# More of the first MoE's opening piece inside the attention's instruction list, with the list and the piece groups rearranged

## The chip, the cores and the metric

The program runs on one core of one Trainium2 chip. The metric is device time in microseconds, the median of the runs of one program; lower is better. Before the change three runs gave 1019.2 to 1020.21 us with a median of 1019.82 us.

## What is computed

The inputs are double precision. An attention over 4 batches, 8 heads, 576 positions and head size 64 comes first, then two feed-forward layers over the 2304 tokens:

```python
bias = -(cum[:, :, :, None] - cum[:, :, None, :])
scores = np.where(causal, -1e9, scores + np.minimum(bias, 0.0))
attn = softmax(scores); x = attn @ v            # 2304 tokens x 512
x = (sigmoid(x @ w_gate) * (x @ w_val)) @ w_out   # MoE 1: 512 -> 1536 -> 512
h = x @ w_in; out = (h * np.cos(h)) @ w2_out      # MoE 2: 512 -> 2048 -> 512
```

## The kernel before, in words

Every product of the two MoE layers is made of three float32r matmuls (`mm3`, lines 390 to 393): high half by high half, high by low, low by high. So each activation and each weight is kept as a high and a low tile. The weights come as doubles; a piece of 128 columns (or rows) is fetched (L302) and decoded by `piece_ops`: VectorE takes out the exponent (L306) and the mantissa (L314, L318), adds the sign (L322) and makes the high half (L332), ScalarE shifts the exponent (L310), GpSimd joins them (L326) and makes the low half (L336).

**Attention.** The 32 heads are worked as 16 pairs p = 0 to 15, four pairs to a batch. The steps of a pair are scores (A), mask (Z, ZA, ZM, on GpSimd mostly), row minimum (X, VectorE, L694), exponential (E, ScalarE, L698), transposes (T, TensorE, L481), copies of them (C, ScalarE or VectorE), the product with v (V, TensorE, L768 and L770), its copy out (U), the reciprocal of the row sums through DRAM (RA, RC, RT, RR, RD, RB), the division (M) and the split into `XH` (XH) and `XL` (XL). All of it, with the decoding of the first three weight pieces (w0, w1, w2), stands in one hand-ordered list, the string `SEQ`: each word is a step, a letter behind the colon the engine that takes it (a: ScalarE, d: VectorE, p: GpSimd). Each engine runs its steps in the order of the list. `Plan.run` (L200 on) gives the PSUM banks while it goes through the list; PSUM has eight banks, and nearly all steps of the attention take two neighbouring ones.

**MoE 1.** Tokens are cut into six blocks of 384. The 12 pieces of 128 hidden columns go in groups (`GROUPS1`, L372); a group runs over all six blocks, and within a block over its pieces. An item (block, piece) has 12 matmuls for the gate, 12 for the value and 12 for the four downs (36 in all). After the last piece of a group each of the four down banks is taken out (`evac1`): in the first group copied to `acc` by ScalarE (L937), in later ones added to it by VectorE (L939). While a group runs, `background` decodes the weight pieces of the next one, a few steps per item. TensorE's order in an item i is: gate and value of i, then the downs of i-1. VectorE's is: multiply value and gate of i (L909), additions of the first two down banks, low half (L917), additions of the other two, decoding.

At the end of the list stand the first parts of MoE 1: gate and value of the first two items (I0 to I15, each three matmuls), the sigmoid chain of the first (Gs, Gm, Gh, Gl) and its four downs (D0 to D3). They sit on fixed banks, all of them among the last steps of pairs 14 and 15. `moe()` goes on with item 2.

Of the kernel before, what the change touches and what calls it, by code (L numbers as in the profile page):

```python
# [10 lines left out]
F32 = mybir.dt.float32  # L11
# [166 lines left out]
WARM = 11  # L178
W0AT = 2
# [18 lines left out]
C0.2.3:d ZA0.5 A3.5 E0.4.4 ZT1.5 HQ6:d ZM0.3.5 C1.2.3:a M1:p E1.2.4 T0.3.4 RT3 GV3 X0.3.5 XH1:p T1.3.4 RR3:a DB6 X1.3.5 GK7 C0.3.4:a ZA1.5 XL1:d A4.5 A0.5 T0.4.4 C1.3.4:a
X1.0.5 X0.0.5 E0.3.5 ZM1.2.5 X1.1.5 RB2 C0.4.4:d V0.3 V1.3 E1.3.5 ZT0.6 X0.1.5 Z1.6:p A2.5 E0.2.4 E1.1.5 ZT1.6 E0.0.5 E0.1.5 T0.2.4 ZM0.2.5 T1.2.4 RA4 Z0.6:p E1.0.5 U3:d
RD3 T0.1.5 ZM0.3.6 ZA1.6 C0.2.4:a ZM1.3.6 X0.2.5 X1.2.5 T0.0.5 A5.5 ZA0.6 RC4 GQ7 PK7 X0.4.5 M2:p C1.2.4:a C0.1.5:a A3.6 RT4 C0.0.5:a T0.3.5 HK7:d DB7 E0.4.5 RR4:d X1.3.6  # L200
T1.3.5 X0.3.6 E0.2.5 A4.6 C0.3.5:a A0.6 X0.1.6 C1.3.5:a T0.4.5 GV5 E1.2.5 A2.6 XH2:p X1.0.6 X1.1.6 ZM1.2.6 ZM0.2.6 RB3 GKT8 RA5 C0.4.5:a X0.0.6 RC5 RD4 T0.2.5 T1.2.5
E1.1.6 XL2:d V0.4 GK8 E0.0.6 Z0.7:p E1.3.6 Z1.7:p E0.1.6 ZT0.7 C0.2.5:d E1.0.6 X1.2.6 X0.2.6 E0.3.6 C1.2.5:d V1.4 U4:a PQ7 T0.0.6 DB8 ZM0.3.7 T0.1.6 C0.1.6:a GQT8 ZA0.7
A5.6 RT5 HQ7:d T0.3.6 T1.3.6 X0.4.6 C0.0.6:a ZT1.7 RR5:d PK8 E0.4.6 A3.7 T0.4.6 HK8:d X0.3.7 M3:p ZA1.7 ZM1.3.7 X1.3.7 w0fetch RB4 C0.3.6:a C1.3.6:a ZM1.2.7 C0.4.6:a A4.7
RD5 E0.2.6 E1.2.6 A0.7 E1.3.7 X0.1.7 PQ8 XL0:p Z1.8:p GQ9 X1.0.7 GVT8 V0.5 HQ8:d X1.1.7 X0.0.7 E0.1.7 w0exponent V1.5 GV6 XH3:d U5:d E0.3.7 A2.7 E1.1.7 ZM0.2.7 E1.0.7 RA6
Z0.8:p ZM0.3.8 X0.2.7 E0.0.7 T0.2.6 T1.2.6 GQ11 T0.1.7 T0.0.7 ZM1.3.8 X1.2.7 C1.2.6:a C0.2.6:a ZT0.8 A5.7 C0.1.7:a w0mant_hi X0.4.7 ZT1.8 PK9 RC6 HK9:a C0.0.7:d A3.8
X0.3.8 RT6 T0.3.7 M4:p E0.4.7 T1.3.7 DB9 GV7 PQ9 X1.3.8 RR6:a C0.3.7:a ZA1.8 ZA0.8 A4.8 E0.3.8 A0.8 C1.3.7:d w0mant_lo E0.2.7 X1.0.8 X1.1.8 ZM1.2.8 X0.0.8 X0.1.8 V0.6
T0.4.7 E1.2.7 HQ9:a XL3:p GK11 E1.1.8 E0.0.8 w0rebias GQ10 Z0.9:p E0.1.8 T0.2.7 w0sign Z1.9:p C0.4.7:d ZM0.2.8 T1.2.7 RA7 C0.2.7:d V1.6 C1.2.7:d ZT0.9 E1.0.8 A2.8 ZT1.9
E1.3.8 X0.2.8 RB5 U6:a T0.1.8 ZM0.3.9 T0.0.8 E0.2.8 A5.8 A3.9 X1.2.8 PQ10 X0.4.8 ZA1.9 C0.1.8:a RD6 X0.3.9 ZM1.3.9 C0.0.8:a T0.3.8 ZA0.9 X1.3.9 M5:p T1.3.8 HQ10:a w1fetch
GK10 XH5:p A4.9 DB10 C1.3.8:d w0add_exp A0.9 E0.3.9 V0.7 E1.3.9 X0.1.9 X0.0.9 X1.1.9 XL5:p X1.0.9 RB6 RC7 XH4:p C0.3.8:d E1.2.8 w0split_hi E0.4.8 E0.1.9 PK10 E1.1.9
# [12 lines left out]
E1.2.12 T0.2.12 XL9:d w1split_hi E0.3.13 ZM0.2.13 E0.0.13 V0.11 E1.0.13 w2fetch X1.2.13 X0.2.13 C0.2.12:d RA12 XH8:d V1.11 w1split_lo M10:p E1.1.13 U11:d T1.2.12 E0.1.13
T0.0.13 C1.2.12:d T0.1.13 A5.13 ZA1.14 X0.4.13 Z1.14:a E0.2.13 E0.4.13 GK15 PQ15 C0.1.13:d DB15 V0.12 w2exponent E1.3.13 HQ15:d RC12 C0.0.13:a E1.2.13 V1.12 XL8:p RT12
T0.4.13 T0.2.13 T1.2.13 w2mant_hi RA13 RR12:d U12:a T0.3.13 RB11 C0.4.13:d ZA0.14 A4.14 Z0.14:p C0.2.13:a A0.14 C0.3.13:a ZT0.15 C1.2.13:d T1.3.13 GV13 ZA0.15 XH10:a RD12
RC13 ZM0.3.14 A3.14 ZT1.15 X0.0.14 X1.1.14 X1.0.14 C1.3.13:a ZM1.3.14 X0.1.14 X1.3.14 X0.3.14 PK15 w2rebias E0.0.14 XL10:p GV14 ZM1.2.14 ZM0.2.14 E1.3.14 V0.13 E0.1.14
HK15:d E1.0.14 w2mant_lo E1.1.14 RT13 A2.14 Z0.15:p V1.13 X1.2.14 E0.3.14 Z1.15:p RR13:a T0.0.14 T0.1.14 X0.2.14 U13:a A4.15 ZA1.15 A0.15 M11:p C0.1.14:a X0.1.15 X1.0.15
# [9 lines left out]
def kernel(  # L236
# [188 lines left out]
    def attention():  # L425
        with ExitStack() as c2:
# [401 lines left out]
            for i, it in enumerate(items1[0:2]):  # L828
# [8 lines left out]
                if i:  # L837
                    continue
# [312 lines left out]
```

## Time and profile before

| what | value |
|---|---|
| median of three runs | 1019.82 us |
| the profiled execution, its own time | 1018.92 us |
| its span (first to last instruction) | 1017.1 us |
| TensorE busy | 1005.4 us, 99% |
| weight loads busy | 913.3 us, 90% |
| VectorE, ScalarE, GpSimd busy | 713.8, 476.2, 408.7 us |
| granted TensorE clock | 0.999 |
| end of the last product with v | 169.75 us into the span |

The program has two stages: the list (the attention), to about 172 us, and the two MoE layers behind it. In the profile a matmul's end is modelled, and one that follows closely overlaps the next; so the distance from one start to the next tells what a matmul costs, not the busy time alone.

### The profile page before, as it was taken

Reading aid. Unit: us, or ns where it says so; the run is one execution under the profiler, and the core shown is the slowest. Engines: PE = TensorE matmul, PEld = TensorE weight load, DVE = VectorE, ACT = ScalarE, POOL = GpSimd, SP = SyncE. Lnnn points to the kernel's source line nnn. Section 1 sums busy time; section 2 is a strip of 40 time slices with the busy share of each in tenths; the row PEclk is TensorE's granted clock in tenths of the full one; section 3 lists DMA queues with packets and bytes.
Section 4 is the critical chain, followed back from the end, with each engine's and each line's share of the span. In section 5 each row is a group of like instructions: output and inputs, shape, how many; then the busy total and the mean of one; then the engine's idle time right before and its main releaser. Section 6 shows DMA issues by size and latency. Waiting matters only on the chain.

```text
span 1017.1 us, 17408 instructions
## 1 busy us (share of the span) xinstructions
PE 1005.4 (99%) x6553; PEld 913.3 (90%) x6553; DVE 713.8 (70%) x1369; ACT 476.2 (47%) x1079; POOL 408.7 (40%) x484
## 2 busy tenths in 40 slices
PE   8999999999999999999999999999999999999998
PEld 5666668999999999999999999899999999999997
DVE  7789885956556577633435878987688888876665
ACT  6998986522122122222112345665555455454453
POOL 5477875532212223311111225555255536552222
PEclk9999999999999999999999999999999999999999
DMA  8988762311111112201001121111012101100011
GB/s 185 201 200 208 189 157 78 103 56 48 44 42 42 42 60 65 64 21 39 24 21 42 42 63 53 52 63 42 22 42 63 42 21 53 52 1 32 32 63 62
DMA packets 91509, 69.43 MB, mean 68 GB/s; under 512 B 58849, under 2 KB 79713, under 8 KB 91425
## 3 DMA queue, kind: packets, MB, share of 16 engines
q1 hardware_dynamic: 89792, 67.86, 24.1%
q8 instruction: 51, 0.84, 0.3%
q10 hardware_dynamic: 1632, 0.47, 0.2%
q14 instruction: 34, 0.27, 0.1%
HBM read 63.45 MB, written 4.87 MB: 67 GB/s over the span
## 4 chain that ended last, share of the span: by engine, by line
PE 85%; DVE 2%; ACT 1%; issue 1%; DMA 0%; POOL 0%; DVEq 0%; POOLq 0%; ACTq 0%
PE pw L391 21%; PE pw L392 21%; PE pw L393 21%; PE pw L992 6%; PE pw L991 6%; PE pw L993 6%; PE pw L770 1%; PE pw L481 1%; PE pw L658 1%; PE pw L663 1%; DMA raw<-in_moe_w_gate_dram 0%; DVE pu L694 0%; DVE wm L314 0%; ACT pu L698 0%; DVE wx L306 0%
## 5 line engine op out<-in xcount | busy, mean ns | idle before, releaser
L391 PE MATMUL pw<-XH,wp 128*128 128x384 f32 x960 | 322.9, 336 | 0.0
L392 PE MATMUL pw<-XL,wp 128*128 128x384 f32 x960 | 322.7, 336 | 0.0
L393 PE MATMUL pw<-XH,wp 128*128 128x384 f32 x960 | 322.6, 336 | 0.0
L336 POOL TENSOR_TENSOR wp<-wm,wp 128x512 fp32r<-128x512 f32 x68 | 100.9, 1483 | 222.1 <-DVE wp L332 218.5
L391 PEld LDWEIGHTS pw<-XH,wp 128*128 128x128 f32 x960 | 180.1, 188 | 4.0
L392 PEld LDWEIGHTS pw<-XL,wp 128*128 128x128 f32 x960 | 180.0, 188 | 3.6
L393 PEld LDWEIGHTS pw<-XH,wp 128*128 128x128 f32 x960 | 180.1, 188 | 0.0
L326 POOL TENSOR_TENSOR wm<-wm,wx 128x512 int32<-128x512 int32 x68 | 90.5, 1331 | 176.3 <-DVE wm L322 175.5
L981 POOL TENSOR_TENSOR gpb<-tmb,gpb 128x384 fp32r<-128x384 f32 x72 | 82.8, 1150 | 110.4 <-ACT gpb L980 110.4
L909 DVE TENSOR_TENSOR tmb<-pw,tmb 128x384 f32<-128x384 f32 x57 | 31.7, 556 | 114.0 <-PE pw L393 111.6
L310 ACT ACTIVATE wx<-wx,ebias 128x512 int32<-128x512 int32 x68 | 49.3, 725 | 92.6 <-DVE wx L306 91.5
L698 ACT ACTIVATE pu<-pu,nm 128x256 f32<-128x256 f32 (+4 forms) x144 | 83.2, 582 | 5.9 <-DVE nm L694 5.7
L992 PE MATMUL pw<-wp,gpb 128*128 128x512 f32 x216 | 84.1, 389 | 0.0
L991 PE MATMUL pw<-wp,gpb 128*128 128x512 f32 x216 | 84.1, 389 | 0.0
L993 PE MATMUL pw<-wp,gpb 128*128 128x512 f32 x216 | 84.0, 389 | 0.0
L391 PE MATMUL pw<-gpb,wp 128*128 128x384 f32 x216 | 72.6, 336 | 1.0 <-ACT acc L937 1.0
L392 PE MATMUL pw<-gpb,wp 128*128 128x384 f32 x216 | 72.9, 337 | 0.0
L393 PE MATMUL pw<-gpb,wp 128*128 128x384 f32 x216 | 72.2, 334 | 0.0
L322 DVE SCALAR_TENSOR_TENSOR wm<-raw,wm 128x512 int32<-128x512 int32 x68 | 69.1, 1017 | 1.5
L960 ACT ACTIVATE tmb<-pw 128x384 int32<-128x384 f32 x96 | 46.6, 485 | 37.6 <-PE pw L393 37.4
L911 ACT CAST gpb<-tmb 128x384 fp32r<-128x384 f32 x43 | 22.1, 514 | 88.7 <-DVE tmb L909 88.7
L908 ACT ACTIVATE tmb<-pw 128x384 f32<-128x384 f32 x57 | 27.8, 488 | 72.4 <-PE pw L393 72.3
(134 smaller groups left out, 1889.9 us busy)
## 6 DMA issues: line engine op xcount, KB each, us to landing
raw<-in_moe_w_out_dram SPq DMA_DIRECT2D x28, 512.0 KB, 3.5
CB<-cum_d SPq DMA_DIRECT2D x15, 576.0 KB, 4.5
raw<-in_moe_w_in_dram SPq DMA_DIRECT2D x16, 512.0 KB, 3.7
raw<-in_moe_w_gate_dram SPq DMA_DIRECT2D x12, 512.0 KB, 3.4
raw<-in_moe_w_val_dram SPq DMA_DIRECT2D x12, 512.0 KB, 3.4
rb<-rec_d SPq DMA_DIRECT2D x32, 144.0 KB, 3.3
out_dram<-acc SPq DMA_DIRECT2D x17, 256.0 KB, 2.1
Kn<-in_k_dram SPq DMA_DIRECT2D x16, 256.0 KB, 5.8
```

What stands on the lines that cost most here:

```text
L310: act.activation(x, x, AF.Relu, bias=ebias[e], scale=8.0)
L322: dve.scalar_tensor_tensor(m, st["raw"][:, :, 1], -2**31, m, ALU.bitwise_and, ALU.bitwise_or)
L326: pool.tensor_tensor(m, m, st["x"], ALU.add)
L336: pool.tensor_tensor(w[:, 1], st["m"].bitcast(F32), f(w[:, 0]), ALU.subtract)
L391: pe.matmul(ps, wh, xh, start=first, stop=False)
L392: pe.matmul(ps, wh, xl, start=False, stop=False)
L393: pe.matmul(ps, wl, xh, start=False, stop=last)
L698: act.activation(o, o, AF.Exp, bias=NMT[nm.slot][:, col:col + 1], scale=-1.0, accum_out=SUMS[sums.slot][:, col:col + 1])
L981: pool.tensor_tensor(gl, g, f(gh), ALU.subtract)
L991: pe.matmul(ps, gh[:, ts], w[:, 0], start=it["first"], stop=False)
L992: pe.matmul(ps, gh[:, ts], w[:, 1], start=False, stop=False)
L993: pe.matmul(ps, gl[:, ts], w[:, 0], start=False, stop=it["last"])
```

## The change

Gate and value of the first four items instead of two, and the downs of the first two instead of one, now stand in the list, scattered from pair 12 on. They take single free PSUM banks that the plan gives out, not fixed ones. The list is ordered anew as a whole. The gate of these four items is made with `Exp`, an addition and a reciprocal on VectorE, not with `Sigmoid`. The tiles for the high and low halves (`GH`, `GL`) lie where the attention's q and k were, and are made once the last of these has been transposed. The last pair takes its reciprocals in a tile of `pt` and not in `rb`; the tail of v has one tile, not two. `GROUPS1` has seven groups: the second one has a single piece. In `moe()` items 2 and 3 start with their splits and downs, on the banks that the list's downs leave, and item 4 makes gate and value of chunks 0 to 2 first and of chunk 3 last. `acc`, `tma`, `tmb`, `gpa` and `gpb` become tiles of their own per block or slot.

```diff
+NI = 4
-    GROUPS1 = [[0], [1, 2], [3, 4], [5, 6], [7, 8, 9], [10, 11]]
+    GROUPS1 = [[0], [1], [2, 3], [4, 5], [6, 7], [8, 9], [10, 11]]
...
-            for i, it in enumerate(items1[0:2]):
-                i_ps = Buf(pl["pw"], 2, 2 * i)
+            for i, it in enumerate(items1[0:NI]):
+                ig, iv = Buf(pl["pw"], 1), Buf(pl["pw"], 1)
...
-                    act.activation(g, it["ps"][0], AF.Sigmoid)
+                    act.activation(g, PW[:, ig.slot, 0:it["n"]], AF.Exp, scale=-1.0)
+                def glu_m(u, it=it, g=TM[i], iv=iv):
+                    dve.tensor_scalar(g, g, 1.0, None, ALU.add)
+                    dve.reciprocal(g, g)
+                    dve.tensor_tensor(g, PW[:, iv.slot, 0:it["n"]], g, ALU.mult)
...
+                if i == NI:
+                    for ks in (range(NDC - 1), [NDC - 1]):
+                        for ps, z in ((pg, "g"), (pv, "v")):
+                            xmm(ps, W[z, it["f"]], it["o"], it["n"], ks)
...
                 if i == 0:
                     ahead()
+                    for k, x in enumerate(items1[2:NI]):
+                        glu(x)
+                        glu_lo(x)
+                        for z, (y, c, _) in enumerate(downs[4 * k:4 * k + 4]):
+                            evac1(items1[y], c, z % 2)
+                    for k, x in enumerate(items1[2:NI]):
+                        for c in range(NDC):
+                            down1(x, c)
+                        for c in range(NDC):
+                            evac1(x, c, c % 2)
+                        if k == 0:
+                            background(5)
```

TensorE at pair 12, before: the transpose of the reciprocals of pair 10 (`rc`), then scores (`K`, `Q`), transposes (`pu`) and the product with v (`pt`, `VN`).

```order
L481 MATMUL pw<-ident,rc 9x64 x2
L658 MATMUL pw<-K_83,Q_81 128x512 x2
L481 MATMUL pw<-ident,pu_104 128x64 x10
L663 MATMUL pw<-K_83,Q_81 128x288 x2
L658 MATMUL pw<-K_83,Q_81 128x128 x2
L658 MATMUL pw<-K_83,Q_81 128x256 x2
L768 MATMUL pw<-pt_105,VN_108 64x64 x2
```

The same place in the change (`wp` is a weight tile; L393 to L395 are the three matmuls of a part of MoE 1).

```order
L395 MATMUL pw<-XH,wp 128x384
L488 MATMUL pw<-ident,rc 9x64 x2
L488 MATMUL pw<-ident,pu_109 128x64 x10
L669 MATMUL pw<-K_89,Q_87 128x288 x2
L664 MATMUL pw<-K_89,Q_87 128x128 x2
L664 MATMUL pw<-K_89,Q_87 128x256 x2
L590 MATMUL pw<-ident,Kn_94 128x64 x8
L590 MATMUL pw<-ident,Kt 128x64 x2
L393 MATMUL pw<-XH,wp 128x384
```

Parts of MoE 1 now stand between the steps of pair 12; before, the first of them stood among the last steps of pairs 14 and 15. Over the whole list they came in five runs on TensorE (4, 5, 2, 5 parts and the 4 downs) and come in nine now (3, 5, 4, 1, 3, 13, 3 parts, 1 down, 7 downs).

TensorE at the end of the list, before: the products with v of the last two pairs (`pt_105`, `pt_106`), then the downs (`gpa`).

```order
L770 MATMUL pw<-pt_106,VN_108 64x448 x2
L770 MATMUL pw<-pt_105,VN_107 64x320 x2
L770 MATMUL pw<-pt_105,VN_107 64x192 x2
L770 MATMUL pw<-pt_105,vt_110 64x64 x2
L770 MATMUL pw<-pt_106,VN_108 64x320 x2
L770 MATMUL pw<-pt_106,VN_108 64x192 x2
L770 MATMUL pw<-pt_106,vt_110 64x64 x2
L391 MATMUL pw<-gpa,wp 128x384
```

And in the change:

```order
L488 MATMUL pw<-ident,rc 9x64 x2
L393 MATMUL pw<-gh_2651,wp 128x384
L394 MATMUL pw<-gl_2655,wp 128x384
L395 MATMUL pw<-gh_2651,wp 128x384
L774 MATMUL pw<-pt_111,VN_113 64x64 x2
L776 MATMUL pw<-pt_111,VN_113 64x512 x2
L776 MATMUL pw<-pt_111,VN_113 64x448 x2
L776 MATMUL pw<-pt_111,VN_113 64x320 x2
L776 MATMUL pw<-pt_111,VN_113 64x192 x2
L776 MATMUL pw<-pt_111,vt 64x64 x2
L393 MATMUL pw<-gh_2651,wp 128x384
```

One down stands before the last product with v and seven behind it; the product of pair 14 has moved up. Ahead of the last product with v stood 48 matmuls of MoE 1; now 99 stand there (96 and 3).

VectorE in the second group of MoE 1, before (`tmb<-pw` is the multiplication, `acc` the additions, `wx`, `wm` and `wp` are decoding):

```order
L909 TENSOR_TENSOR tmb<-pw,tmb 128x384
L939 TENSOR_TENSOR acc<-pw,acc 128x384 x2
L917 TENSOR_TENSOR gpa<-tmb,gpa 128x384
L939 TENSOR_TENSOR acc<-pw,acc 128x384 x2
L306 TENSOR_SCALAR wx<-raw 128x512
L314 TENSOR_SCALAR wm<-raw 128x512
L909 TENSOR_TENSOR tmb<-pw,tmb 128x384
L917 TENSOR_TENSOR gpb<-tmb,gpb 128x384
L332 CAST wp<-wm 128x512
```

And in the change:

```order
L936 TENSOR_TENSOR tm_65<-pw,tm_65 128x384
L969 TENSOR_TENSOR acc_3148<-pw,acc_3148 128x384 x2
L944 TENSOR_TENSOR gl_2655<-tm_65,gh_2651 128x384
L969 TENSOR_TENSOR acc_3148<-pw,acc_3148 128x384 x2
L320 SCALAR_TENSOR_TENSOR wm<-raw,wm 128x512
L324 SCALAR_TENSOR_TENSOR wm<-raw,wm 128x512
L308 TENSOR_SCALAR wx<-raw 128x512
L316 TENSOR_SCALAR wm<-raw 128x512
L334 CAST wp<-wm 128x512
L320 SCALAR_TENSOR_TENSOR wm<-raw,wm 128x512
L936 TENSOR_TENSOR tm_3137<-pw,tm_3137 128x384
```

In this group every item now ends with four additions, where every second one did, and six decoding steps stand between one item's and the next, where there were two or three.

## Rows read from the trace of the kernel before

**Rows 1.** The page, the chain that ended last, by engine.

```profile
PE 85%; DVE 2%; ACT 1%; issue 1%; DMA 0%; POOL 0%; DVEq 0%; POOLq 0%; ACTq 0%
```

**Rows 2.** Windows; columns: stretch, length, PE, PEld, DVE, ACT, POOL busy, clock, DMA.

```profile
10.00:60.00 50.00, 47.35 (x624) 31.38 (x622) 40.56 (x134) 44.52 (x140) 27.29 (x84) 1.00 0.88 200
60.00:115.00 55.00, 53.16 (x692) 33.82 (x690) 48.27 (x149) 49.66 (x150) 43.07 (x88) 1.00 0.89 208
115.00:150.00 35.00, 34.63 (x440) 22.02 (x436) 29.75 (x96) 31.02 (x91) 27.89 (x57) 1.00 0.62 161
150.00:172.00 22.00, 21.96 (x211) 17.14 (x210) 14.19 (x31) 15.84 (x41) 9.25 (x10) 1.00 0.17 50
172.00:198.00 26.00, 25.26 (x144) 24.58 (x143) 20.49 (x30) 13.28 (x29) 13.72 (x10) 1.00 0.37 117
...
210.00:600.00 390.00, 390.00 (x2250) 390.00 (x2249) 223.21 (x417) 93.37 (x176) 89.39 (x64) 1.00 0.14 44
```

**Rows 3.** Timeline of PE in the list; columns: start, us, engine, line, operation, count.

```profile
139.31 1.11 PE L481 MATMUL pw<-ident,pu 64*128 64x64 f32 x30
140.24 0.72 PE L663 MATMUL pw<-K,Q 64*128 64x288 f32 x4
...
150.22 0.71 PE L481 MATMUL pw<-ident,pu 64*128 64x64 f32 x16
150.90 0.45 PE L391 MATMUL pw<-XH,wp 128*128 128x384 f32 x1
151.18 0.34 PE L392 MATMUL pw<-XL,wp 128*128 128x384 f32 x1
...
152.91 0.34 PE L393 MATMUL pw<-XH,wp 128*128 128x384 f32 x1
153.18 0.59 PE L481 MATMUL pw<-ident,pu 64*128 64x64 f32 x12
```

**Rows 4.** Timeline of PE: last product with v, and MoE 1's first group.

```profile
169.47 0.28 PE L770 MATMUL pw<-pt,vt 128*64 128x64 f32 x4
...
182.10 0.34 PE L393 MATMUL pw<-XH,wp 128*128 128x384 f32 x1
183.18 0.44 PE L391 MATMUL pw<-gpb,wp 128*128 128x384 f32 x1 [0.74 <-ACT acc L937]
...
208.44 0.34 PE L393 MATMUL pw<-XH,wp 128*128 128x384 f32 x1
209.03 0.44 PE L391 MATMUL pw<-gpb,wp 128*128 128x384 f32 x1 [0.25 <-ACT acc L937]
209.42 0.44 PE L392 MATMUL pw<-gpb,wp 128*128 128x384 f32 x1
```

**Rows 5.** Timeline of DVE in the first group, two stretches of six decoding steps.

```profile
189.80 0.68 DVE L318 SCALAR_TENSOR_TENSOR wm<-raw,wm 128x512 int32<-128x512 int32 x1
...
193.84 0.55 DVE L909 TENSOR_TENSOR tmb<-pw,tmb 128x384 f32<-128x384 f32 x1
...
195.44 0.68 DVE L322 SCALAR_TENSOR_TENSOR wm<-raw,wm 128x512 int32<-128x512 int32 x1
...
200.46 0.55 DVE L909 TENSOR_TENSOR tma<-pw,tma 128x384 f32<-128x384 f32 x1
```

**Rows 6.** Groups by form, 172 to 600 us: additions, low halves of weights.

```profile
L939 DVE TENSOR_TENSOR acc<-pw,acc 128x384 f32<-128x384 f32 x96 | 49.6, 550 | 0.0
...
L336 POOL TENSOR_TENSOR wp<-wm,wp 128x512 fp32r<-128x512 f32 x38 | 57.4, 1511 | 178.5 <-DVE wp L332 177.1 <-PE pw L393 1.4
```

**Rows 7.** Timeline: table load in the list; behind it the first decoding step, last XL.

```profile
159.27 1.28 ACT L842 ACT_TABLE_LOAD   x1
...
176.48 0.43 DVE L306 TENSOR_SCALAR wx<-raw 128x512 int32<-128x512 int32 x1 [3.05 <-DMA raw<-in_moe_w_gate_dram]
...
176.57 1.65 POOL L812 TENSOR_TENSOR XL<-w,XH 128x576 fp32r<-128x576 f32 x1
```

More of the change, by code (lines that the diff above doesn't have):

```diff
@@ L282 @@
     XL = base.tile([P, NDC, NT], F32R, name="XL")
-    TMA = base.tile([P, TB], F32, name="tma")
-    GPA = base.tile([P, 2 * TB], F32R, name="gpa")
+    TM = [base.tile([P, TB], F32, name=f"tm{i}") for i in range(NI)]
+    GH, GL = [], []
     w0ring = ctx.enter_context(tc.tile_pool(name="w0ring", bufs=3))
@@ L420 @@
     items1, items2 = work(GROUPS1, BLOCKS), work(GROUPS2, BLOCKS)
+    downs = []
     def attention():
@@ L440, in attention @@
             VN = [att.tile([P, NT4, 2, D], F32, name=f"VN{i}") for i in range(NV)]
-            VT = [att.tile([P, PB, 2, D], F32, name=f"vt{i}") for i in range(2)]
+            VT = att.tile([P, PB, 2, D], F32, name="vt")
             WT = [att.tile([P, S], F32, name=f"w{i}") for i in range(NW)]
@@ L513, in setup_tail @@
                     u.memset(PU[4][i][:, S:NQ * P], 0.0)
-                for i in range(2):
-                    u.memset(VT[i][TAIL:P], 0.0)
+                u.memset(VT[TAIL:P], 0.0)
             add("cum", "dve:1850", setup_cum, wr=["cum"], at=2.85)
@@ L867, in attention @@
+                    add(f"D{i}.{c}", "pe:520", down, rd=[("gh", i), ("gl", i), ("W", 2, 0), ("W", 2, 1)], wr=[d_ps])
+            left = {f"PQ{NP - 1}", f"PK{NP - 1}"}
             for o in plan.run(SEQ):
                 o.fn()
+                if o.name[0] == "D" and o.name[1:2].isdigit():
+                    downs.append((*(int(x) for x in o.name[1:].split(".")), o.bufs[0].slot))
+                left.discard(o.name)
+                if not left and not GH:
+                    qkst.close()
+                    gp = ctx.enter_context(tc.tile_pool(name="gp", bufs=1, side="right", reuse_waits="tile"))
+                    GH.extend(gp.tile([P, TB], F32R, name=f"gh{i}") for i in range(4))
+                    GL.extend(gp.tile([P, TB], F32R, name=f"gl{i}") for i in range(4))
@@ L880, in moe @@
             rings.append(c2.enter_context(tc.tile_pool(name="ring", bufs=13, reuse_waits="tile")))
-            acc = accp.tile([P, NDC * NT], F32, name="acc")
+            accs = [accp.tile([P, NDC * TB], F32, name=f"acc{b}") for b in range(NB)]
             class Slots:
@@ L918, in glu_lo @@
                 it["g"] = gh, gl
-            late = []
+            late, PW8, free = [], psums["all"], [z for i, c, z in downs]
             def down1(it, c):
@@ L1066, in moe @@
                     flush()
-                    group = [x for x in items1 if x["gi"] == it["gi"]][1:]
+                    group = [x for x in items1 if x["gi"] == it["gi"]][min(it["gi"], 1):]
                     room, given = [0.0], 0
```

247 lines of the change are left out of this document (131 added, 116 removed).

## The prediction

> **What bounds the kernel now.** I read the chain first: 85% of the span is TensorE [rows 1], so the question is where TensorE has time that is not work. The windows tell that by stage. From 210 us on PE and PEld are both busy for the whole 390.00 us: there a matmul costs 390.00 / 2250 = 0.1733 us, and nothing waits [rows 2]. In the list it is nearly the same picture: of the 35 us from 115 to 150 PE is without work for 0.37 us, of the 22 us behind it for 0.04, of the 105 us from 10 to 115 for 2.65 + 1.84 = 4.49 us [rows 2]. ScalarE comes next, with 49.66 of 55 and 31.02 of 35. Modelled ends hide short pauses, so I looked at starts in the timeline: 30 transposes from 139.31 take 0.93 us to the next step, 31 ns each, and 16 from 150.22 take 0.68, 42 ns each, of which 16 x 31 = 0.50 is work; so a run of transposes can hide 0.18 us [rows 3]. A reader should see from this that the attention is bound by TensorE as the MoE layers are, with little idle time to fill, most of it before pair 12.
>
> **The change, part by part.** The sum is made against the profiled execution's own 1018.92 us (span 1017.1), which is 0.9 below the median of 1019.82; I carry the difference over to the median.
>
> *Work moved into the list.* 51 more matmuls stand ahead of the last product with v: 51 x 0.1733 = 8.8 us. They are only moved: as many fewer follow. On a TensorE that is full in both stages this changes nothing by itself; the end of the last product with v goes from 169.75 us (169.47 + 0.28 [rows 4]) to some 178, and the rest is shorter by as much. What it can win is idle time between 115 and 150 us, since the parts of blocks 0 to 2 become ready about there: at least 0 (the parts may meet no pause), at most 0.37 shown plus 0.18 in each of the 13 runs of transposes that the timeline has there, 2.7 us. From 150 on parts of MoE 1 stood there already, and 0.04 us is left [rows 2], so such parts do fill what they meet; but they must fall where the pause is. I take half: -1.4.
>
> *More runs.* A run of MoE parts costs on entry 0.28 us from its first matmul to its second (150.90 to 151.18) in place of 0.17, and on exit 0.27 (152.91 to 153.18) in place of 0.17 [rows 3]: 0.2 us a run. Five runs become nine: +0.8.
>
> *Stalls of the first group that go.* Behind the list TensorE waited for ScalarE's copies of the down banks: 182.10 to 183.18 (0.90 over a matmul's time), 208.44 to 209.03 to 209.42 (0.41 and 0.22) [rows 4]. Copies now alternate between two engines for four of the six blocks, and decoding for a group of one piece halves the steps of VectorE that held up the chain: -1.5. If they stay, it is 0.
>
> *The joint item.* Its chunk 3 needs the last pair's XL, which ended at 178.22, 8.5 us behind the last product with v [rows 7, 4]. In the change 7 downs, 8 downs and the joint's first 18 matmuls stand between: 21 + 24 + 18 matmuls of 0.1733, 10.9 us. That covers it by 2.4 us even if the last pair's reciprocals arrive no earlier; they go to a tile of their own and may arrive sooner. Cost 0; without that cover it would be the difference.
>
> *Weights of the second group.* Their first decoding step began at 176.48, 6.7 us behind the last product with v [rows 7]; the fetch hangs on the same queue and I leave it there. The value weights of piece 1 are wanted when item 6 has made its gate: 21 + 24 + 24 + 36 + 12 = 117 matmuls, 20.3 us behind it. VectorE reaches their high half only behind the multiplication and low half of item 5, whose value ends at 93 matmuls, 16.1 us; the two and the copy between them take about 1.6, two decoding steps 0.8 to 1.8, and GpSimd's low half 1.5 [rows 5, 6]: 20.0 to 21.0, later by up to 1.3 if the first Sigmoid's table load, 1.28 us long and in the list before [rows 7], holds up item 4. Needed at 20.65 (the third matmul). So 0 to 1.7 us; I take the middle, +0.9.
>
> *The second group's VectorE.* With one piece in the group each item needs a multiplication, a low half and four additions, 0.55 long each [rows 5, 6], some 0.47 from start to start, 2.8 us, and six decoding steps: 4.04 us between 189.80 and 193.84, 5.02 between 195.44 and 200.46 [rows 5]. That is 6.9 to 7.8 us in an item of 36 x 0.1733 = 6.24 us: VectorE falls behind by 0.6 to 1.6 us an item, for the five items that decode, 3.1 to 8 us in all. An item's low half can be ready 4.2 us before its downs want it (estimate: the 24 + 12 + 24 matmuls from the start of its gate, less the 24 and the 2.0 us of steps up to it), so the first 4.2 us cost nothing. Then 0 to 3.8 us; I take +1.0, since some of the slow decoding steps met GpSimd, and the additions now stand between the two. The additions themselves, 24 more, lie beside matmuls.
>
> *The rest of the list.* It is ordered anew and its divisions and splits move from VectorE and ScalarE to GpSimd, which is at 43.07 of 55 us [rows 2] at its fullest. At most it gains the 4.49 us of idle time from 10 to 115 [rows 2], and it may lose as much: the steps are the same and no row says which. I take 0 and keep both ends. The Exp chain adds some 4 us to VectorE in the list, beside TensorE's work, where VectorE has 14.19 of 22 us busy at the end [rows 2].
>
> Here the Trainium skill speaks otherwise. PEld is busy for 22.02 of 35 us before 150 and 24.58 of 26 behind the list [rows 2]. The page "Perfetto Trace Analysis", section "Identifying the Most-Contended Engine", says that the busy share of matmuls is a poor measure of how full TensorE is and that of the weight loads a good one; by that the list has 13 us to fill before 150 and the moved work would be free. The starts speak against it: the attention's matmuls use half of the rows and follow one another without a pause [rows 3], with loads that are short beside them.
>
> Sum: -1.4 + 0.8 - 1.5 + 0.9 + 1.0 = -0.2 us: 1018.7 for the profiled execution, **1019.6** as a median. What a measurement of this kernel can tell from no change is about 0.2%, 2 us; the forecast is no change.
>
> **The rivals.**
>
> *The list closes up* (faster). The new order takes half of the idle time before 115 us (2.5) and all of the 2.7 behind it, and the new stalls are 0.5: -2.7 + 0.8 - 1.5 + 0.5 - 2.5 = -5.4, **1014.4**. For it: TensorE's waits there are few and long enough to be ordered away. Against: the parts that could fill them come only from pair 12 on. Chance 0.25.
>
> *TensorE is emptier than it looks* (faster). The moved 8.8 us are all hidden: -8.8 + 0.8 - 1.5 + 1.9 = -7.6, **1012.2**. For it the loads' share, against it the starts. Chance 0.09.
>
> *VectorE bounds the second group* (slower). The place is items 7 to 11, the decision whether six decoding steps take more than about 4.2 us there (6.24 + 4.2 / 5 - 2.8). At the slow end of the row, 5.02, the stall is 3.8 and the late value weights 1.7: 2.8 + 0.8 above the forecast, **1023.2**. For it the rows, against it that VectorE waited for ScalarE between some of them. Chance 0.15.
>
> *The list runs out of banks* (slower). Parts on single banks hold one of the four bank pairs through pairs 12 and 13, two at the end. A wait for a copy out of a bank cost 0.90 [rows 4]; one in each of four pairs makes 3.6: **1023.2**. Against it: in the list ScalarE and VectorE empty banks as soon as they are full. Chance 0.11.
>
> **How the numbers follow.** No change has 0.40: the sum lies near 0, and its terms are of both signs and at most some 3 us. Faster gets 0.25 + 0.09 = 0.34, slower 0.15 + 0.11 = 0.26. The range leaves out the second rival and the slowest tail: 1012.5 to 1024.5. The likeliest case alone spans 1017.8 to 1021.9.
>
> **What would show it.** Right: the last product with v ends at 177 to 179 us; PE is full from 115 us to its end; no wait above 0.2 us between it and item 6; in the second group VectorE is busy for over 9.5 of 10 us, with a wait of TensorE there of about 1 us in all. Wrong: the last product ends before 174 (the list had room, or closed up before pair 12) or behind 181 (banks); TensorE waits for low halves or additions in the second group by over 3 us.

## The result, and the profile after

The change makes the kernel slower: 1035.05 us (median of 6 runs, 1031.86 to 1038.34) against 1019.87 us (6 runs, 1019.2 to 1021.53), a ratio of 1.0145, interval 1.0123 to 1.0166. The forecast was 1019.6 us with a range to 1024.5; the time lies 10.5 us above that range. The profiled execution took 1035.35 us, with a span of 1033.6 us, 16.5 us more than that of the kernel before.

The chain that ended last, from the page of the changed kernel, answers to [rows 1]: VectorE has gone from 2% to 8% of it, and the DMA from nothing to 3%.

```profile
PE 84%; DVE 8%; DMA 3%; POOL 2%; issue 1%; ACT 1%; POOLq 0%; DVEq 0%; SPq 0%; ACTq 0%
```

The windows of the changed kernel (columns as in [rows 2]) tell it by stage.

```profile
10.00:60.00 50.00, 48.01 (x630) 31.18 (x630) 42.45 (x141) 44.55 (x137) 26.59 (x80) 1.00 0.80 188
60.00:115.00 55.00, 52.25 (x686) 33.97 (x686) 45.36 (x136) 47.80 (x143) 43.58 (x86) 1.00 0.84 205
115.00:150.00 35.00, 32.11 (x360) 23.73 (x358) 24.45 (x73) 29.24 (x84) 22.30 (x47) 1.00 0.66 170
150.00:172.00 22.00, 21.57 (x217) 15.99 (x219) 17.48 (x47) 14.83 (x44) 14.95 (x26) 1.00 0.20 53
182.00:198.00 16.00, 13.34 (x81) 12.73 (x78) 13.42 (x21) 7.52 (x14) 8.78 (x7) 1.00 0.36 118
210.00:600.00 390.00, 389.34 (x2217) 388.77 (x2216) 236.03 (x440) 91.85 (x173) 94.46 (x69) 1.00 0.15 47
```

A reader sees idle time of TensorE that was not there: 2.89 us between 115 and 150 us (0.37 before), 2.66 behind the list. The last row looks harmless, since PE is busy for all but 0.66 us of 390. But count its matmuls: 2217, where [rows 2] have 2250. Less the 0.66 us, one costs 389.34 / 2217 = 0.1756 us in place of 0.1733. A busy TensorE has become slower, and no wait tells of it.

The timeline of PE, answering to [rows 3, 4] (start, us, line, operation, and in brackets the idle time and what ended it):

```profile
79.38 1.23 PE L488 MATMUL pw<-ident,pu 64*128 64x64 f32 x24 [1.49 <-DVE K L481]
...
149.94 0.53 PE L488 MATMUL pw<-ident,pu 64*128 64x64 f32 x10 [1.56 <-DVE nm L700]
...
182.31 0.28 PE L776 MATMUL pw<-pt,vt 128*64 128x64 f32 x4
...
184.57 0.34 PE L395 MATMUL pw<-gh,wp 128*128 128x384 f32 x1
187.57 0.45 PE L393 MATMUL pw<-gh,wp 128*128 128x384 f32 x1 [2.66 <-DVE tm L856]
...
205.87 0.33 PE L395 MATMUL pw<-XH,wp 128*128 128x384 f32 x1
206.85 0.44 PE L393 MATMUL pw<-XH,wp 128*128 128x384 f32 x1 [0.65 <-DVE wp L334]
207.13 0.34 PE L394 MATMUL pw<-XL,wp 128*128 128x384 f32 x1
208.57 0.44 PE L395 MATMUL pw<-XH,wp 128*128 128x384 f32 x1 [1.10 <-POOL wp L338]
...
255.38 0.43 PE L393 MATMUL pw<-gh,wp 128*128 128x384 f32 x1 [0.25 <-ACT gh L938]
256.22 0.45 PE L394 MATMUL pw<-gl,wp 128*128 128x384 f32 x1 [0.41 <-DVE gl L944]
```

The sum of the loss, from these rows: the last product with v ends at 182.59 us, where 169.75 and 51 moved matmuls give 178.59: 4.0 us. Behind it TensorE waits for a multiplication of the gate (L856): 187.57 - 184.57 less a matmul, 2.8. The value weights of piece 1 are late: 0.81 + 1.27 = 2.1. The second group has two short waits around 255 us, 1.1 in all. The first group's old stalls, 1.5, are gone. That makes 8.5 of 16.5 us; the other 8.0 are the slower matmuls, about 1.9 ns in each of some 2,500 in MoE 1 (4.7 us; 300.00 / 1712 less 300.00 / 1731 in the windows further down, which hold no wait), and the rest in MoE 2. Of the 4.0 us ahead of the last product with v, 3.2 are more idle time in the windows: 0.25 up to 115 us, 2.52 up to 150 and 0.39 behind that.

Behind two of the waits stands one line. The timeline of DVE in the changed kernel, one gate in the middle of the list and the last two at its end:

```profile
144.45 0.36 DVE L854 TENSOR_SCALAR tm<-tm 128x384 f32<-128x384 f32 x1
144.84 2.55 DVE L855 RECIPROCAL tm<-tm 128x384 f32<-128x384 f32 x1
147.49 0.56 DVE L856 TENSOR_TENSOR tm<-pw,tm 128x384 f32<-128x384 f32 x1
148.11 0.69 DVE L700 CUSTOM_DVE_ANT_0 pu<-pw,CB 128x512 f32<-128x512 f32 x1
...
149.10 0.68 DVE L700 CUSTOM_DVE_ANT_0 pu<-pw,CB 128x512 f32<-128x512 f32 x1
...
178.19 1.57 DVE L854 TENSOR_SCALAR tm<-tm 128x384 f32<-128x384 f32 x1
179.79 2.55 DVE L855 RECIPROCAL tm<-tm 128x384 f32<-128x384 f32 x1
182.45 0.56 DVE L856 TENSOR_TENSOR tm<-pw,tm 128x384 f32<-128x384 f32 x1
182.93 1.34 DVE L854 TENSOR_SCALAR tm<-tm 128x384 f32<-128x384 f32 x1
184.30 2.55 DVE L855 RECIPROCAL tm<-tm 128x384 f32<-128x384 f32 x1
186.96 0.56 DVE L856 TENSOR_TENSOR tm<-pw,tm 128x384 f32<-128x384 f32 x1
```

A reciprocal of 128x384 takes 2.55 us, 4.6 times as long as the multiplication behind it. The chain in the middle stands ahead of the row minima (L700) that the transposes at 149.94 wait for; the two at the end run one behind the other, and the second multiplication ends at 187.52, 2.8 us after TensorE ran out of work (184.57 and a matmul).

What TensorE waits for in both places is a PSUM bank. The down at 187.57 takes halves that GpSimd had made by 153.3 us; in the program it writes bank 1, from which the last multiplication reads its value. The transposes at 149.94 write banks 4 and 5, from which the row minima at 149.10 and 148.11 read their scores. The slow step holds a bank, or delays the step behind it that would free one.

### The profile page after: what moved, and what is told of

Same layout as the page of the kernel before. It is cut to its first block, busy times and chain, and to the rows that moved or that the text cites. A ratio compares the mean times of both kernels' runs of the same rounds, so it can differ in the third digit from the quotient of the medians.

```text
span 1033.6 us, 17459 instructions
## 1 busy us (share of the span) xinstructions
PE 1014.5 (98%) x6553; PEld 916.9 (89%) x6553; DVE 740.4 (72%) x1401; ACT 474.5 (46%) x1069; POOL 415.8 (40%) x493
## 4 chain that ended last, share of the span: by engine, by line
PE 84%; DVE 8%; DMA 3%; POOL 2%; issue 1%; ACT 1%; POOLq 0%; DVEq 0%; SPq 0%; ACTq 0%
PE pw L395 19%; PE pw L393 19%; PE pw L394 19%; PE pw L1023 6%; PE pw L1022 6%; PE pw L1021 6%; PE pw L664 2%; PE pw L776 2%; PE pw L488 2%; DMA CB<-cum_d 1%; PE pw L669 1%; DVE acc L969 1%; DVE pu L700 1%; DVE wm L316 1%; DVE tm L855 1%
## 5 line engine op out<-in xcount | busy, mean ns | idle before, releaser
L395 PE MATMUL pw<-XH,wp 128*128 128x384 f32 x960 | 323.3, 337 | 1.1 <-POOL wp L338 1.1
L393 PE MATMUL pw<-XH,wp 128*128 128x384 f32 x960 | 323.6, 337 | 0.7 <-DVE wp L334 0.7
L393 PEld LDWEIGHTS pw<-XH,wp 128*128 128x128 f32 x960 | 180.3, 188 | 6.6 <-DVE wp L334 1.0
L395 PEld LDWEIGHTS pw<-XH,wp 128*128 128x128 f32 x960 | 179.9, 187 | 1.4 <-POOL wp L338 1.4
L1011 POOL TENSOR_TENSOR gl<-tm,gh 128x384 fp32r<-128x384 f32 x96 | 106.0, 1104 | 150.9 <-ACT gh L1010 150.7
L936 DVE TENSOR_TENSOR tm<-pw,tm 128x384 f32<-128x384 f32 x68 | 37.8, 556 | 135.3 <-PE pw L395 129.3
L1023 PE MATMUL pw<-wp,gl 128*128 128x512 f32 x288 | 114.4, 397 | 0.0
L1022 PE MATMUL pw<-wp,gh 128*128 128x512 f32 x288 | 114.0, 396 | 0.0
L1021 PE MATMUL pw<-wp,gh 128*128 128x512 f32 x288 | 113.8, 395 | 0.0
L996 DVE SCALAR_TENSOR_TENSOR tm<-tm,tm 128x384 f32<-128x384 int32 x96 | 105.1, 1095 | 3.3
L997 ACT ACTIVATE tm<-tm 128x384 f32<-128x384 f32 x96 | 50.5, 526 | 114.7 <-DVE tm L996 114.7
L393 PE MATMUL pw<-gh,wp 128*128 128x384 f32 x288 | 97.9, 340 | 2.9 <-DVE tm L856 2.7
L394 PE MATMUL pw<-gl,wp 128*128 128x384 f32 x288 | 97.6, 339 | 0.4 <-DVE gl L944 0.4
L395 PE MATMUL pw<-gh,wp 128*128 128x384 f32 x288 | 97.5, 338 | 0.0
L704 ACT ACTIVATE pu<-pu,nm 128x512 f32<-128x512 f32 (+4 forms) x144 | 83.3, 583 | 12.1 <-DVE nm L700 11.7
L1004 DVE SCALAR_TENSOR_TENSOR tm<-tm,pw 128x384 f32<-128x384 f32 x96 | 52.7, 548 | 42.6 <-ACT tm L998 42.6
```

Of the source, the lines that this page charges most:

```text
L393: pe.matmul(ps, wh, xh, start=first, stop=False)
L394: pe.matmul(ps, wh, xl, start=False, stop=False)
L395: pe.matmul(ps, wl, xh, start=False, stop=last)
L704: act.activation(o, o, AF.Exp, bias=NMT[nm.slot][:, col:col + 1], scale=-1.0, accum_out=SUMS[sums.slot][:, col:col + 1])
L996: dve.scalar_tensor_tensor(r, kk, -TWO_PI_LO, r, ALU.mult, ALU.add)
L1004: dve.scalar_tensor_tensor(g, r, -0.5, h, ALU.add, ALU.mult)
```

## Experiments: why the matmuls are slower

**The new tiles lie 32 bytes off a multiple of 64.** GH and GL begin at byte 217056 of a partition, 32 off a multiple of 64; the tiles that they replace (GPA at 91776, GPB at 113344) lay on one. XH, XL and the weights stand as before against a multiple of 256. The first run moves GH and GL alone.

```diff
                     GL.extend(gp.tile([P, TB], F32R, name=f"gl{i}") for i in range(4))
+                    gp.tile([P, 8], F32, name="gpad")
```

> The changed kernel with an unused tile of 32 bytes per partition behind the four GH and four GL tiles, which moves these from byte 217056 of a partition to 217024, a multiple of 64; nothing else changes. Placement theory: the matmuls of both MoE layers became slower (173.5 to 175.3 ns in MoE 1, 227.5 to 233.9 for the 128x512 ones in MoE 2) because GH and GL begin 32 bytes off a multiple of 64; then they come back to 173 to 174 and about 227 ns, and the time falls by some 8 us, to 1026 to 1028. Rival (the rate comes from the PSUM banks, from other engines' traffic or from the order): the rates stay and the time stays at 1035 +- 1.

Measured: 1027.37 us (1024.31 to 1027.79), ratio to the kernel before 1.0072 (1.0056 to 1.0087): 7.7 us less than the change for an unused tile of 32 bytes. The same 300 us of MoE 1 (windows, columns as before) hold 1731 matmuls in the kernel before, 1712 in the changed one, 1731 in this one. First the kernel before, then the changed one, then this one:

```profile
300.00:600.00 300.00, 300.00 (x1731) 300.00 (x1730) 172.87 (x321) 72.80 (x137) 70.46 (x51) 1.00 0.14 45
```

```profile
300.00:600.00 300.00, 300.00 (x1712) 300.00 (x1711) 171.86 (x325) 69.31 (x131) 65.18 (x49) 1.00 0.14 43
```

```profile
300.00:600.00 300.00, 300.00 (x1731) 300.00 (x1730) 175.39 (x329) 70.07 (x132) 67.87 (x49) 1.00 0.14 44
```

**The same in the kernel before.** Three runs move the halves there: GPA and GPB by 32 bytes, by 64 bytes (tiles 64 bytes longer in both, so the weights move too, by 64 and 128), and GPB alone by 32 in a tile 256 bytes longer, with which all else keeps its place against a multiple of 256.

```diff
-    GPA = base.tile([P, 2 * TB], F32R, name="gpa")
+    GPA = base.tile([P, 2 * TB + 16], F32R, name="gpa")[:, 8:8 + 2 * TB]
...
-            GPB = mid.tile([P, 6 * TB], F32R, name="gpb")
+            GPB = mid.tile([P, 6 * TB + 16], F32R, name="gpb")[:, 8:8 + 6 * TB]
```

> The kernel before with GPA and GPB (high and low halves of the gated values) begun 32 bytes later in a tile that is 64 bytes longer, so that they start 32 off a multiple of 64; what lies behind them moves by 64 and 128 bytes. Placement theory: its MoE matmuls take on the rates of the changed kernel (about 175 ns, and 233 for 128x512): some 8 us slower, 1027 to 1029. Rival: no change, 1019 to 1021.

> Control: the same longer tiles, but GPA and GPB begin 64 bytes later, on a multiple of 64; all else lies where the run shifted by 32 has it. Placement theory with 64 bytes as the grain: 1019 to 1021. If any shift counts (their place against the weights or a coarser grain): as slow as the run shifted by 32.

Measured: 1020.9 us (1.0015; 1.0006 to 1.0025) and 1018.61 us (0.9991; 0.9982 to 1.0001). The direction was right, the size not: 8 us were expected of the first. MoE 2's 128x512 matmuls did slow down, from 227.5 ns from start to start to 233.3, but its 128x384 ones went from 176.6 to 174.1, and both runs had moved the weights. So the third run:

```diff
-            GPB = mid.tile([P, 6 * TB], F32R, name="gpb")
+            GPB = mid.tile([P, 6 * TB + 64], F32R, name="gpb")[:, 8:8 + 6 * TB]
```

> The kernel before with GPB alone begun 32 bytes later, in a tile 256 bytes longer, so that weights, x and GPA keep their place against a multiple of 256 and GPB (three of four of the gated halves) stands as GH and GL do in the change. Run before_by32 also moved the weights, and cost 1.3 us in place of 8. Placement theory: with the weights where they were, the rates of the change come back: MoE 2's 128x512 matmuls of GPB from 226.7 to 233 or 234 ns (620 of them, +4 us), MoE 1's to 175 to 176.5 (+4), MoE 2's 128x384 ones from 176.6 to 174.6 (-2): 1024 to 1026. Rival (the loss of 7.7 us needs the change's program, not the place alone): as before_by32, 1019.5 to 1021.

Measured: 1029.4 us (1027.01 to 1032.25), 1.0104 (1.0082 to 1.0126): one tile, moved by 32 bytes, costs the kernel before 9.4 us. That is more than the 1024 to 1026 expected: MoE 2's 128x384 matmuls stayed at 176.5 ns, where a gain of 2 us had been counted in, and GPA's 128x512 ones slowed as well, from 229.9 to 232.9. Its window holds as few matmuls as that of the change, and in the groups by form from 650 to 1000 us the 128x512 matmul of GPB takes 394 ns (second fence) where it takes 389 in the kernel before (third).

```profile
300.00:600.00 300.00, 300.00 (x1717) 300.00 (x1716) 171.44 (x317) 71.67 (x135) 70.90 (x50) 1.00 0.14 45
```

```profile
L991 PE MATMUL pw<-wp,gpb 128*128 128x512 f32 x186 | 73.3, 394 | 0.0
L992 PE MATMUL pw<-wp,gpb 128*128 128x512 f32 x186 | 73.3, 394 | 0.0
```

```profile
L991 PE MATMUL pw<-wp,gpb 128*128 128x512 f32 x189 | 73.5, 389 | 0.0
```

The place of the halves is a cause by itself, shown from both sides. What in the chip makes it so was not found: the matmuls of XH slow down too (173.2 to 175.2 ns in MoE 1), though XH, XL and their weights keep their places, and the rates depend on both operands.

## Experiments: the reciprocals, the weights, the list

**Tanh for the reciprocal.** 0.5 tanh(x / 2) + 0.5 needs one ScalarE step and a short one of VectorE; it stands alone, and then with the 32-byte tile.

```diff
-                    act.activation(g, PW[:, ig.slot, 0:it["n"]], AF.Exp, scale=-1.0)
+                    act.activation(g, PW[:, ig.slot, 0:it["n"]], AF.Tanh, scale=0.5)
...
-                    dve.tensor_scalar(g, g, 1.0, None, ALU.add)
-                    dve.reciprocal(g, g)
+                    dve.tensor_scalar(g, g, 0.5, 0.5, ALU.mult, ALU.add)
```

> The changed kernel with the gate in the list as 0.5 x Tanh(x / 2) + 0.5 (one ScalarE activation, one VectorE step) in place of Exp, addition and reciprocal; same order and places. Reciprocal theory: four steps of 2.55 us on VectorE leave the list, TensorE's wait of 2.8 us behind the tail's two chains (184.6 to 187.6 us) and most of the 1.6 us behind the chain at 145 to 149 us go: 1035 - 4 = 1030 to 1032. Rival (the list is slower because of its new order and its banks, the chain lies beside TensorE's work): less than 1 us, 1034 to 1035.

> Both edits of the first two runs together: the 32-byte tile that puts GH and GL on a multiple of 64, and Tanh in place of Exp, addition and reciprocal. If the two causes are independent, the savings add: 1035 - 7.7 - 4.3 = 1023 (1022 to 1024), with matmul rates as in the kernel before and no wait of TensorE between the last product with v and the second group; left would be the late value weights at the second group's start (2.1 us) and two waits some 45 us behind (1.5 us). If they hide each other: 1025 to 1027.

Measured: 1030.77 us (1.0117; 1.0086 to 1.0148), 4.3 us less than the change, and 1022.36 us with both (1.0029; 1.0016 to 1.0043): 12.7 less, where 7.7 + 4.3 = 12.0. The two savings add up. The waits at 187.57 (2.66 us) and at 149.94 (1.56) are gone in both traces, 4.2 us together. The four runs of after_tanh lie between 1027.77 and 1035.91, and the profiled one is the slowest, with a granted clock of 0.50 from 123 to 126 us, the lower level, 1.2 GHz; so the single saving is known to about 2 us. From after_aligned to after_both it is 5.0.

**Which group decodes what.** The groups of the kernel before in after_both, and the change's seven groups in the kernel before.

```diff
-    GROUPS1 = [[0], [1], [2, 3], [4, 5], [6, 7], [8, 9], [10, 11]]
+    GROUPS1 = [[0], [1, 2], [3, 4], [5, 6], [7, 8, 9], [10, 11]]
```

> after_both with the groups of the kernel before ([0], [1, 2], [3, 4], ...), so that MoE 1's first group decodes two pieces in place of one. Theory: the first group behind the list is now 8.8 us shorter, so its VectorE is late with the weights of two pieces by more than with those of one; the wait at the second group's start grows from 2 to 4 us or more, 1025 to 1027, though the waits 45 us behind go. Rival (the second group with one piece is what costs the rest): the waits go, 1019 to 1021.

> The kernel before with nothing but the change's seven groups ([0], [1], [2, 3], ...). By the prediction's term for the second group's VectorE (one piece, six decoding steps an item): TensorE waits there for 0 to 3.8 us and no wait for weights at its start, since the first group is long here; the first group's stalls of 1.5 us get shorter: 1018.5 to 1022. If the groups explain what is left of the change's loss (3.6 us): 1023.

Measured: 1030.52 us for the first (1.0113; 1.0081 to 1.0145), more than either side expected, and 1019.72 for the second (0.9997; 0.9985 to 1.0009). In the kernel before, the single-piece group brings waits of 1.7 us at 238 to 247 us and takes the first group's stalls away; the two cancel. In the change it is needed: with two pieces to decode, TensorE waits in the shortened first group for copies of its down banks (L967), which stand on ScalarE behind decoding steps that each wait 3.7 to 4.0 us for VectorE. Windows of both_groups:

```profile
201.00:207.00 6.00, 0.26 (x2) 0.00 (x0) 4.16 (x7) 1.81 (x4) 3.20 (x3) 0.90 0.51 168
207.00:213.00 6.00, 5.77 (x19) 5.77 (x20) 5.96 (x9) 2.42 (x6) 3.40 (x3) 0.53 0.27 76
```

TensorE waits for 6.1 us, and then runs for 6 us at a granted clock of 0.53, almost all of it at the lower level of 1.2 GHz: 19 matmuls where 34 fit. This second loss, 15 matmuls or 2.6 us, is most of the 3.5 us by which it came out beyond the expectation.

**The late value weights.** Ten decoding steps ahead of item 4's gating instead of five (both_early), or twelve by the end of item 4 (both_twelve), both on top of after_both.

```diff
-                            background(5)
-                            given += 5
+                            background(10)
+                            given += 10
```

> after_both with ten instead of five of the second group's decoding steps between the first group's downs (background(10)), so ahead of item 4's multiplication, where VectorE stands idle for 2.4 us; item 4 then has none and item 5 five as now. Theory: the two waits for the late value weights (1.23 + 1.27 us) go: 1022.4 - 2.5 = 1020, within 0.2% of the kernel before; what is left is the two waits of the second group (1.5 us) and the list. Rival: the steps delay item 4's multiplication and low half and TensorE waits for these: no gain.

Measured: 1023.19 us (1.0038; 1.0026 to 1.005), no gain: the rival was right. The two waits went and another came, for the copies (L967) of the last two banks of the first group's downs: on ScalarE these stand behind a decoding step that waits for VectorE. First PE, then ACT of both_early:

```profile
194.93 0.44 PE L393 MATMUL pw<-XH,wp 128*128 128x384 f32 x1 [3.10 <-ACT acc L967]
...
196.21 0.53 PE L393 MATMUL pw<-XH,wp 128*128 128x384 f32 x1
196.53 0.53 PE L394 MATMUL pw<-XL,wp 128*128 128x384 f32 x1
```

```profile
193.79 0.72 ACT L312 ACTIVATE wx<-wx,ebias 128x512 int32<-128x512 int32 x1 [3.72 <-DVE wx L308]
194.42 0.84 ACT L967 COPY acc<-pw 128x384 f32<-128x384 f32 x2
```

Here too the clock falls behind a wait: from 195 to 199 us the granted clock is 0.62, and at the lower level, 1.2 GHz, the matmuls start 0.32 us apart in place of 0.17.

```diff
                     share = {id(x): math.ceil(total * r / room[-1]) for x, r in zip(group, room[1:])}
+                    if it["g0"]:
+                        share[id(items1[NI])] = 12
```

> after_both with 7 instead of 5 decoding steps behind item 4's gating (12 of the 15 by then), so that the high half of the value weights stands ahead of item 5's multiplication, where VectorE waited 1.2 us for ScalarE, and the copies of banks keep their place. Theory: the waits for the value weights (2.5 us) go and no other comes: 1020. Rival: item 5's multiplication or another wait takes their place: 1022 to 1023, as after_both.

Measured: 1019.51 us against 1019.66 for the kernel before beside it (12 and 17 runs), 1.0001 (0.9991 to 1.001). The copies keep their place, the weights come in time, and no new wait follows; the two short ones of the second group stay (0.47 and 0.41 us, at 247). With its three costs taken away the change moves the time by nothing that can be measured. The last product with v ends at 179.53 us here, 0.9 behind the 178.59 that the moved work alone gives. TensorE is as full ahead of it as in the kernel before, 34.63 of 35 us, though with fewer and longer matmuls:

```profile
115.00:150.00 35.00, 34.63 (x395) 25.72 (x394) 23.37 (x78) 31.25 (x89) 24.16 (x53) 1.00 0.66 165
```

**Do the parts fill anything?** The parts of MoE 1 are taken out of the list and put behind its last product with v, with the order of the change (on after_both) and with that of the kernel before. The edit is in the list's words alone.

```diff
-... V1.13 ... I0.4 X0.1.15 I0.5 I0.6 E0.3.15 ... D0.1 ... V0.15 ... V1.15 RD15 D0.2 ... D1.3
+... V1.13 ... X0.1.15 E0.3.15 ... V0.15 ... V1.15 RD15 XL14:p RB15 I0.0 I0.1 ... Gm3 D0.0 ... D1.3
```

> after_both with the words of MoE 1's 32 gate and value parts, their gating and 8 downs taken out of the list's middle and put behind the last product with v, in one run; the rest of the new order stays. If the parts win nothing inside the list (TensorE is full there, they are only moved), the last product with v ends earlier by their 99 matmuls, 17 us (at some 166 us), and the time is within 1 us of after_both. If they fill idle time, it is slower by what they fill (2 to 4 us); if they disturb the list (banks, runs), faster by 1 to 3 us.

> The kernel before with MoE 1's 16 gate and value parts, their gating and 4 downs taken out of the list and put behind the last product with v, the rest of its order unchanged. The prediction held that TensorE is full in the list: then the last product with v ends earlier by its 48 matmuls of 0.173 us, at 169.8 - 8.3 = 161.5 us, and the time stays within 1 us or grows by the gating's latency (2 to 3 us). If the list's last third is paced by ScalarE and VectorE, and the parts fill what they leave: it ends at 165 to 168 us and the time grows by as much, 4 to 7 us.

Measured: 1037.37 us (1.0176; 1.0158 to 1.0193) and 1026.31 us (1.0063; 1.005 to 1.0077); the last product with v ends at 177.11 and 170.9 us, not at 166 and 161.5. So without parts the end of the list is not TensorE's, in either order. both_late is 15.0 us slower than after_both, more than any side expected: without the parts TensorE is idle in the new order for 5.7 of the 35 us before 150 and for 5.8 of the 27.1 behind, and the granted clock there is 0.95 and 0.87. Windows and groups of before_late:

```profile
115.00:150.00 35.00, 34.66 (x442) 22.26 (x440) 30.12 (x94) 31.57 (x94) 28.98 (x60) 1.00 0.66 169
150.00:172.00 22.00, 15.79 (x165) 9.38 (x164) 11.99 (x33) 13.99 (x40) 8.71 (x11) 0.84 0.17 53
```

```profile
L481 PE MATMUL pw<-ident,rc 64*9 64x64 f32 x12 | 1.4, 228 | 5.8 <-DVE rc L780 5.7
```

In the old order TensorE is full to 150 us without any part. Behind that the last two pairs wait for their reciprocals (5.7 us), and the clock falls to 0.84. The kernel before fills just that stretch with its 48 matmuls; 51 more find nothing there, which is what both_twelve shows.

**The weights moved by 128 bytes.** From the rates of the first runs, weights at byte 64 of 256 should speed up MoE 2's 128x384 matmuls. All tiles behind the first ones move by 128 bytes; in before_128:

```diff
     GPA = base.tile([P, 2 * TB], F32R, name="gpa")
+    base.tile([P, 32], F32, name="gap")
```

> both_early with all tiles behind the first five moved by 128 bytes (weights and GH, GL at byte 64 of 256 in place of 192). Placement as the first runs show it: MoE 2's 128x384 matmuls go from 176.6 to 173.4 ns (1,100 of them, -3.5 us), its 128x512 ones from 226.7 to 228.3 (860, +1.4), MoE 1's downs from 174.2 to 175.2 (860, +0.9): 1 to 1.5 us faster than both_early, 1018.5 to 1019. If rates do not follow from the places: any other value.

> The kernel before with everything behind GPA moved by 128 bytes: weights at byte 64 of 256, GPB at 64, GPA at 128 as it was. By the same rates: MoE 2's 128x384 matmuls 176.6 to 173.4 (-3.4 us), the 128x512 ones of GPB 226.7 to 228.3 (+1.0), MoE 1's downs +0.7: 1.5 to 2 us faster, 1017.5 to 1018, if GPA's pair of places (64 against 128) is no worse than before's.

Measured: both_early_128 1021.89 us (1.0023; 1.0011 to 1.0036), 1.3 less than both_early. That is the difference expected, but the intervals of the two overlap, and since both_early had not come down to 1020, neither did this come to 1018.5 or 1019. before_128 takes 1018.23 us, 0.9987 (0.9978 to 0.9995). The 128x384 matmuls went from 176.6 to 173.4 ns as expected; 1.0 us was won where 1.5 to 2 were expected, and GPA's 128x512 matmuls became slower (229.9 to 232.9 ns). It is the lowest median of all, just clear of noise.

## Why the prediction was wrong, point by point

- **A matmul costs 0.1733 us** (the first paragraph, and every count in the sum). This step failed, by 7.7 us of the 15.2. It was read from [rows 2] and carried over to a program whose tiles lie elsewhere; the section on the change says that GH and GL take the attention's old place, and the sum has no term for it. No rival had it either.
- **"The Exp chain adds some 4 us to VectorE in the list, beside TensorE's work."** This step failed, by about 4.3 us. The four chains take 16.1 us, 10.2 of it in reciprocals: I had set a wide reciprocal near the other steps, which take 0.55, though none stood in the trace, and should have bounded it. Nor is it all beside TensorE's work, since VectorE frees the banks that TensorE writes next: one chain stands ahead of row minima, two at the end have no cover left. The Trainium skill says why such a step is no ordinary one: the page "VectorE: DVE Perf Modes", section "First, the fixed hardware budget", describes the reciprocal as an iterated divide with a repeat count of 8. 2.55 us against the 0.56 of the multiplication fits that.
- **The value weights, 0 to 1.7 us, taken as 0.9.** The mechanism was right, the size too small: 2.1 us, and 2.5 in after_both, beyond the upper bound. The value weights' steps stood behind item 5's multiplication as forecast; both_twelve moves them ahead of it, and the wait goes.
- **The second group's VectorE, 0 to 3.8, taken as 1.0.** Right: 1.1 us, and 1.7 in before_groups. The rival that made it 3.8 fell.
- **More runs, +0.8.** It fits, though no run isolates it: both_twelve, with the idle time of the kernel before from 10 us on (5.0 and 4.9 us), ends the last product with v 0.9 behind the moved work.
- **The first group's stalls, -1.5, and the joint item, 0.** Right: no wait for a bank's copy stands behind the list, and none for the last XL.
- **Moved work is neutral.** Right in the end: with the costs above taken away the time is that of the kernel before. The gain of 1.4 us between 115 and 150 was not found as such. TensorE was idle for 2.89 us there, since a chain of the gate and late row minima stood in the way; without the chain, in both_twelve, it was idle for 0.37 as before, so this term is 0. And "the attention is bound by TensorE as the MoE layers are" holds to 150 us alone: behind that TensorE is idle for 6.2 us when no parts stand there (before_late, in the old order).
- **The rest of the list, 0 with ends of 4.5.** Up to 115 us the 0 was right: TensorE is idle for 4.74 us from 10 to 115, where it was for 4.49, so the rival that the list closes up fell as well. The new order has a wait at 79.38, 40 us ahead of the first part, but others went. Yet the last product with v ended at 182.59, beyond my sign for "wrong" at 181. TensorE does wait for banks, as the rival of the banks had it; ahead of that product scores hold them, at 187.57 a value of MoE 1, and each time VectorE reads them late: "in the list ScalarE and VectorE empty banks as soon as they are full" is what failed. 1.56 us is the chain ahead of the row minima, gone in all six traces with Tanh, whose banks are the same. Another 1.11 is a wait for row minima at 120.77, which four of the eight traces with this list have (0.81 to 1.42 us) and four have not. The end lies between 178.0 and 183.3 us in these eight, and between 178.0 and 180.9 in the five with Tanh and full clock.
- **TensorE is emptier than it looks** (0.09). It fell for the stretch to 150 us, which in the old order is full with no part in it, and the loads' share [rows 2] was the wrong sign there.

## What to carry to other kernels

When a change moves tiles, compare where their operands start before and after, and count matmuls per window in a stage that the change doesn't touch: a slower rate on a full engine shows in no wait and no busy share. Price every instruction form that the trace of before doesn't hold by bounds from both sides, a wide reciprocal above all, and look for what stands behind it on its engine and at the PSUM banks that it keeps from TensorE meanwhile. When a wait is moved away, look at what the moved steps now stand ahead of on each queue.

## What the runs showed of the hardware

- The start of a matmul's operand changes what matmuls cost, by up to 3% here: 128x512 ones took 226.7 ns from start to start with both operands at byte 192 of 256, and 233 or 234 with the gated half at byte 224. Neighbours that don't touch that tile slow down with it by 1%: in before_gpb32 those of XH from 173.2 to 175.2 ns, those of GPA from 229.9 to 232.9. That such kernels scatter more is not shown: before_by32, with its halves 32 bytes off, lies within 1.6 us in 10 runs, and after_both, with its halves on a multiple of 64, within 5.9.
- A wait of TensorE of 3.1 us (both_early) and one of 6.1 us (both_groups) were each followed by matmuls at 1.2 GHz; one of 2.7 us (187.57 above) was not. The length of the wait alone does not tell: in after_tanh a wait of 1.4 us that ends at 121.40 is followed by a granted clock of 0.50 from 123 to 126 us.
- One TENSOR_SCALAR of 128x384 takes 0.36 us alone (144.45) and 1.57 at 178.19, where GpSimd runs a 1.44 us subtraction from 178.11. The Trainium skill has a reason to offer: in "GPSIMD Engine Reference", section "1. Specifications", GpSimd shares its SBUF interfaces with VectorE and contends with VectorE's instructions in a two-port mode or with two SBUF inputs. The two rows fit that; in which mode the step ran, no run here shows.
